# Decode attention with paired key/value heads: fixed on-chip buffers, values one step behind keys, keys turned by column quarters

## The chip, the cores and the metric

The kernel runs on one core of a Trainium2 chip. The metric is the device time of one launch in microseconds (us). Engines of the core that matter here: PE (TensorE, matmuls), DVE (VectorE), ACT (ScalarE), POOL (GpSimd) and SP (SyncE), whose instruction stream issues nearly all the DMAs. Sixteen DMA engines carry the transfers from the chip's memory (HBM) into the on-chip memory (SBUF); matmul results land in PSUM.

## The reference

One decode step. Eight batches, each with one token of width 512, 32 query heads and 8 key/value heads of width 128, a cache of 8192 tokens. All in float32. The sum of three parts is returned:

```python
xn = _layernorm(x)
return x + _A_ref(xn, A_k_cache, A_v_cache, A_wq, A_wo) + _B_ref(xn, B_w1, B_b1, B_w2, B_b2)

# A: grouped-query attention over the cache, four query heads to a key/value head
q = (x @ wq) ...
scores = einsum("bhqd,bhkd->bhqk", q, k) * Dh ** -0.5
o = einsum("bhqk,bhkd->bhqd", softmax(scores), v)
return o ... @ wo

# B: a token-mixing MLP with one token: per batch, 512 channels x 1792 hidden units
u = gelu(einsum("bsd,sf->bdf", layernorm(x), w1) + b1)
return einsum("bdf,fs->bds", u, w2) + b2
```

The two caches are 8 x 8 x 8192 x 128 float32 each, 268 MB for K and as much for V; every byte is read once. The weights wq and wo are 8.4 MB each.

## The kernel before

**Tiles.** The eight key/value heads of each batch are worked on in two ways. Heads 0 to 5 go in pairs: a "duo" is one batch and two neighbouring heads, 24 of them (`N_PR`), and its K and its V are 8.4 MB each, laid out as 128 partitions x 64 KB (64 partitions to a head, each with 128 consecutive tokens). Heads 6 and 7 go one by one: 16 single tiles of 4.2 MB for K and for V each (128 partitions x 32 KB). `slots` (L56) is the buffer for all of them: five slots (`RING`) of 32 KB per partition, so a duo tile takes two slots and a single tile one.

**Slots before.** `slot(n)` (L59) hands the five slots out in a ring, in the order of the loads. A duo tile whose turn comes at the last slot is split: one half in slot 4, one half in slot 0. The weight wq comes first: its main part (`body`) lies in slots 0 and 1, the rest (`extra`) in slot 4.

**Loads.** `load_next` (L184) issues the next load: first the duos (`load_duo`, L166) in the order K0, V0, K1, V1, ..., then the single heads in the order of the list `order`. A duo's load is one DMA with rows of 64 KB or several with shorter rows: K0 comes in four parts of 16 KB rows, the later K duos up to number 7 in two parts of 32 KB rows, from number 8 (`AHEAD`) in one part except every fifth, V duos in one part, and any duo that is split over slots 4 and 0 in two DMAs of 32 KB rows. All are issued by SP, in order, and SP waits before each one until the slot's last reader is done. POOL issues some small parts of wq at the start (`load_side`), and w1, b1, w2 after them.

**A duo step** (`duo_step`, L697) does for one duo i, in the order in which the engines get their instructions:

1. For each half k of the keys (one slot each) and each half of that half: two transposes on DVE in place (`turn_duo`, L570: a chunk of 16 tokens x 128 columns, contiguous, in 32 x 32 blocks), then eight matmuls (`qk_duo`, L576), each over one chunk and one column quarter of 32, which go over two column groups of PE in turn. After the first half `load_next` is called.
2. `softmax_duo` (L588): row maximum on DVE, its transpose over the partitions on PE, the bias on DVE, exp on ACT, two matmuls with `send` and two DVE transposes that bring the weights into `PT`.
3. `pv_duo(i, 0)`: 16 matmuls with the first half of the values, over four column groups; then `load_next`, two pieces of the mixer MLP (`mix`: ACT gelu, POOL multiply and add), and every fourth step the placing of four finished results (`place_duo`); in two steps of eight a projection with wo and its next load.
4. `pv_duo(i, 1)`, the copy of the result out of PSUM on ACT (`take_duo`), two more mixer pieces, and a small exp on ACT that loads its table.

So a step works on K(i) and V(i) together. Each matmul on float32 shows as two instructions in the profile.

**Single heads.** `pair(i)` (L738) turns the keys of head i, and does QK of the one before and PV of the one before that. The last three are written out by hand; the last V comes in five pieces.

**Start.** wq, K0 and the first part of wo are loaded; DVE turns K0; `q_project` (L377) multiplies with wq, main part first and the rest after it, and `q_place_duo` lays the queries into Z. Then the steps begin.

Of the kernel before, what the change touches and what calls it, by code (L numbers as in the profile page):

```python
# [15 lines left out]
REP = HQ // HKV  # L16
# [23 lines left out]
AHEAD = 8  # L40
# [10 lines left out]
def attn_mixer_kernel(ctx: ExitStack, tc: tile.TileContext, x, kc, vc, wq, wo, w1, b1, w2, b2, out):  # L51
# [5 lines left out]
    taken = [0]  # L57

    def slot(n=1):  # L59
        at = taken[0] % RING  # L60
        taken[0] += n
        return slots[:, at:at + n, :]
# [24 lines left out]
    order.sort(key=lambda o: -o[0])  # L87
    at = [o[1:] for o in order].index((kc, KR, N_IT - 1))
    order[at], order[at + 1] = order[at + 1], order[at]
# [6 lines left out]
    body = slot(2).rearrange("p s m -> p (s m)")  # L96
    extra = slots[:, RING - 1, :]
# [66 lines left out]
    duo = [(src, to, i) for i in range(N_PR) for src, to in ((kc, KP), (vc, VP))][::-1]  # L164

    def load_duo():  # L166
        src, to, i = duo.pop()
        g, b = divmod(i, B)
        rows = src[b, 2 * g:2 * g + 2].rearrange("h (p t) d -> (h p) (t d)", p=HP)
        half = NT * DH  # L170
        if taken[0] % RING < RING - 1:
            t = slot(2).rearrange("p s m -> p (s m)")
            n = 1 if to is VP or i >= AHEAD and i % RING else 2 if i else 4
            for a in range(n):
                x = slice(a * 2 * half // n, (a + 1) * 2 * half // n)
                nc.sync.dma_start(t[:, x], rows[:, x])
            parts = [t[:, k * half:(k + 1) * half] for k in range(2)]
        else:
            parts = [slot().rearrange("p s m -> p (s m)") for _ in range(2)]
            for k in (0, 1) if i else (1, 0):  # L180
                nc.sync.dma_start(parts[k], rows[:, k * half:(k + 1) * half])
        to[i] = [t.rearrange("p (t d) -> p t d", d=DH) for t in parts]

    def load_next():  # L184
        if duo:
            load_duo()
        elif order:
            _, src, to, i = order.pop()
            h, b = divmod(i, B)
            t = slot().rearrange("p s (t d) -> p (s t) d", d=DH)  # L190
            rows = src[b, h].rearrange("(p t) d -> p t d", p=P)
            last = not order
            at = 0
            for n in PIECES if last else (NT,):
                nc.sync.dma_start(t[:, at:at + n, :], rows[:, at:at + n, :])
                at += n
            to[i] = t
            if last:
                load_wo(HKV - 1)
# [20 lines left out]
    yrow = const.tile([W, D], F32, name="yrow")  # L220
    load_next()
# [155 lines left out]
    def q_project():  # L377
        part = [[(lw[:, j, :], body[:, j * WB:(j + 1) * WB]) for j in range(a * WJ // 2, (a + 1) * WJ // 2)] for a in range(2)]
        part.append([(lx[:, j, :], extra[:, j * WB:(j + 1) * WB]) for j in range(WE * NB)])
        ms = [misc(), misc()]  # L380
        n = sum(map(len, part))
        at = 0
        for todo in part:
            for a in range(2):
                for j, (l, w) in enumerate(todo, at):
                    g = j % NB
                    nc.tensor.matmul(ms[a][g * W:(g + 1) * W, :], l, w[:, a * REP * DH:(a + 1) * REP * DH],  # L387
                                     start=(j < NB), stop=(j >= n - NB))
# [181 lines left out]
    def turn_duo(i, c):  # L570
        k = KP[i][c // NCH][:, c % NCH * CH_T:(c % NCH + 1) * CH_T, :].rearrange("p t d -> p (t d)")
        nc.vector.transpose(k, k)  # L572
# [3 lines left out]
    def qk_duo(i, k, cs):  # L576
        b = i % B
        if not k and not cs[0]:
            SD[i] = ps_a.tile([P, 512], F32, name="acc")
        t = KP[i][k]  # L580
        for q in range(NB):
            for c in cs:
                nc.tensor.matmul(SD[i][c * W:(c + 1) * W, :].rearrange("p (t j) -> p t j", j=W),  # L583
                                 Z[:, q, b, (1 - k) * REP:(1 - k) * REP + W],
                                 t[:, c * CH_T:(c + 1) * CH_T, q * W:(q + 1) * W],
                                 start=(not k and not q), stop=(k == 1 and q == NB - 1))

    def softmax_duo(i):  # L588
        b = i % B
        s = SD.pop(i)  # L590
        mr = work.tile([P, 1], F32, name="mr")
        nc.vector.tensor_reduce(mr, s, AX.X, ALU.max)  # L592
# [7 lines left out]
        nc.scalar.activation(p, s, AF.Exp, bias=nb, scale=SCALE, accum_out=LD[i // HB][:, b % HB:b % HB + 1])  # L600
# [88 lines left out]
    for c in range(NCH):  # L689
        turn_duo(0, c)  # L690
# [6 lines left out]
    def duo_step(i):  # L697
        g, b = divmod(i, B)
        half = NCH // 2
        for k in range(2):  # L700
            for x in range(2):
                for c in range(half) if i or k else ():
                    turn_duo(i, k * NCH + x * half + c)
                qk_duo(i, k, range(x * half, (x + 1) * half))
            if not k:
                load_next()
                if i == N_PR - 1:
                    load_next()
        if i == N_PR - 1:
            load_next()  # L710
        del KP[i]
        softmax_duo(i)
        pv_duo(i, 0)
        load_next()
        mix(2)
        if b == B - 1 and g < PAIRED // 2 - 1:
            q_place_duo(g + 1)
        if i:
            place_duo(i - 1)
# [5 lines left out]
        if g and b == 2:  # L725
            load_wo(2 * g)
        pv_duo(i, 1)
        if i == N_PR - 1:
            load_next()
        del VP[i]  # L730
        take_duo(i)
        mix(2)
        nc.scalar.activation(small.tile([P, 1], F32, name="warm"), own[:, :1], AF.Exp)  # L733

    for i in range(N_PR):
        duo_step(i)

    def pair(i):  # L738
# [7 lines left out]
        if i == FIRST:  # L746
            place_duo(N_PR - 1)
            fill_softmax(False, big())
            fill_place(False, big())
# [23 lines left out]
        if step[0] <= B * NF:  # L773
            mix(1)
        if h == PAIRED and b == 1:
            o_project(h - 2)
            load_wo(h - 1)
# [70 lines left out]
    assert not order  # L848
# [27 lines left out]
```

## Time and profile before

| | us |
|---|---|
| median of three timed runs | 1292.58 (1291.95 to 1292.74) |
| span of the profiled execution, first to last instruction | 1290.3 |
| PE busy in it | 931.9 (72%) |
| DVE busy | 712.1 (55%) |
| ACT, POOL busy | 236.6, 235.3 (18% each) |
| bytes moved | 554.43 MB, mean 430 GB/s over the span |
| chain that ended last: DMA, PE, DVE | 58%, 20%, 20% |

How to read it. A row such as "PE" under the slices has one digit for each fortieth of the span: the busy share in tenths, 9 being 90% or more. "Idle before" of a group of instructions is how long its engine stood still ahead of them, with what ended the wait. The chain of waits is followed back from the last instruction, at each step to what released it; a piece of it that is a DMA says only that somebody waited from that DMA's issue to its landing. A transfer that is queued behind another is in that time too.

### The profile page before, as it was taken

How to read it: one execution, taken by the hardware profiler on the slowest of the kernel's cores; microseconds unless marked ns; L12 is line 12 of the kernel's file. 1: busy time of each engine (PE TensorE's matmuls, PEld its weight loads, DVE VectorE, ACT ScalarE, POOL GpSimd, SP SyncE). 2: the span in 40 equal slices, each digit the busy share in tenths (PEclk: the TensorE clock that was granted, in tenths of full speed). 3: DMA queues.
4: the chain of work that ended last, by engine and by line, in shares of the span. 5: the costliest groups of instructions: out<-in, count | busy, mean ns of one | idle time of the engine just before them, and what ended most of it. 6: DMA issues, size and time to landing. Idle time of an engine off the chain costs nothing.

```text
span 1290.3 us, 11358 instructions
## 1 busy us (share of the span) xinstructions
PE 931.9 (72%) x4776; PEld 254.5 (20%) x4776; DVE 712.1 (55%) x645; ACT 236.6 (18%) x348; POOL 235.3 (18%) x254
## 2 busy tenths in 40 slices
PE   4677686877786857786848787857687674766778
PEld 1212121212221211121212111212112111111223
DVE  6654446654446634665625665626566645566575
ACT  1022212122111221111221212220223332310000
POOL 3022212122121221112221212220233311100000
PEclk8888898988988979898989898988898887878889
DMA  9999999999999999999999999999999999999998
GB/s 392 434 438 437 429 426 433 434 432 445 422 436 427 432 443 431 428 440 428 429 443 431 426 441 433 425 439 435 425 433 431 433 431 433 431 435 431 431 435 344
DMA packets 17974, 554.43 MB, mean 430 GB/s; under 512 B 2597, under 2 KB 2629, under 8 KB 3409
## 3 DMA queue, kind: packets, MB, share of 16 engines
q1 hardware_dynamic: 17220, 553.08, 99.4%
q8 instruction: 37, 0.61, 0.2%
q0 software_dynamic: 672, 0.61, 0.1%
q14 instruction: 13, 0.11, 0.0%
q10 hardware_dynamic: 32, 0.02, 0.0%
HBM read 553.69 MB, written 0.02 MB: 429 GB/s over the span
## 4 chain that ended last, share of the span: by engine, by line
DMA 58%; PE 20%; DVE 20%; issue 1%; ACT 1%; SPq 0%; POOL 0%; ACTq 0%; DVEq 0%
DMA raw<-in_A_k_cache_dram 39%; DMA raw<-in_A_v_cache_dram 16%; DVE raw L572 14%; PE acc L615 5%; PE acc L583 5%; DVE raw L428 3%; PE acc L506 3%; DMA raw<-in_A_wq_dram 3%; PE misc L603 1%; PE misc L560 1%; PE acc L439 1%; PE misc L632 1%; PE misc L387 0%; ACT t2k L600 0%; DVE s L638 0%
## 5 line engine op out<-in xcount | busy, mean ns | idle before, releaser
L572 DVE STREAM_TRANSPOSE raw<-raw 128x2048 f32<-128x2048 f32 x192 | 425.1, 2275 | 166.3 <-DMA raw<-in_A_k_cache_dram 166.3
L583 PE MATMUL acc<-raw,z 128*32 128x512 f32 x1536 | 396.3, 640 | 165.3 <-DVE raw L572 159.1
L667 POOL TENSOR_SCALAR g<-g,pad 128x512 f32<-128x512 f32 x112 | 77.5, 692 | 720.1 <-ACT g L666 720.1
L615 PE MATMUL acc<-raw,pt 128*32 128x512 f32 x1536 | 189.4, 633 | 14.2 <-DMA raw<-in_A_v_cache_dram 13.3
L583 PEld LDWEIGHTS acc<-raw,z 128*32 128x32 f32 x1536 | 92.4, 115 | 468.3 <-issue 296.7
L428 DVE STREAM_TRANSPOSE raw<-raw 128x2048 f32<-128x2048 f32 x64 | 145.7, 2293 | 65.8 <-DMA raw<-in_A_k_cache_dram 65.8
L668 POOL TENSOR_TENSOR macc<-macc,g 128x512 f32<-128x512 f32 x112 | 142.1, 1269 | 9.3
L666 ACT ACTIVATE g<-hb,pad 128x512 f32<-128x512 f32 x112 | 87.2, 778 | 145.3 <-POOL macc L668 125.3
L600 ACT ACTIVATE t2k<-acc,nb 128x512 f32<-128x512 f32 x24 | 16.5, 687 | 441.7 <-DVE nb L596 441.6
L439 PE MATMUL acc<-raw,z 128*32 128x512 f32 x512 | 82.9, 650 | 10.8 <-DVE raw L428 8.2
L603 PE MATMUL misc<-t2k,send 128*128 128x512 f32 x96 | 62.4, 785 | 33.3 <-ACT t2k L600 33.3
L615 PEld LDWEIGHTS acc<-raw,pt 128*32 128x32 f32 x1536 | 51.9, 115 | 149.8 <-issue 121.7
L506 PE MATMUL acc<-raw,pt 128*32 128x512 f32 x480 | 75.9, 772 | 0.0
L604 DVE STREAM_TRANSPOSE pt<-misc 128x512 f32<-128x512 f32 x48 | 34.4, 717 | 69.3 <-PE misc L603 67.6
L592 DVE TENSOR_REDUCE mr<-acc 128x1 f32<-128x512 f32 x24 | 16.6, 692 | 89.1 <-PE acc L583 89.1
L456 PE MATMUL misc<-ident,mr 128*128 128x128 f32 x16 | 6.4, 398 | 76.3 <-DVE mr L451 76.3
L666 ACT ACT_TABLE_LOAD x32 | 41.1, 1283 | 29.0 <-PE hb L658 28.5
L623 ACT COPY ob<-acc 128x512 f32<-128x512 f32 x24 | 14.0, 584 | 150.5 <-PE acc L615 150.5
L473 ACT ACTIVATE t2k<-acc,nb 128x512 f32<-128x512 f32 x16 | 11.0, 687 | 134.7 <-DVE nb L462 134.6
L439 PEld LDWEIGHTS acc<-raw,z 128*32 128x32 f32 x512 | 19.5, 117 | 64.0 <-issue 44.8
L733 ACT ACT_TABLE_LOAD x24 | 30.8, 1283 | 0.4
L603 PEld LDWEIGHTS misc<-t2k,send 128*128 128x128 f32 x96 | 19.6, 226 | 52.8 <-ACT t2k L600 37.8
(136 smaller groups left out, 375.8 us busy)
## 6 DMA issues: line engine op xcount, KB each, us to landing
raw<-in_A_k_cache_dram SPq DMA_DIRECT2D x44, 4096.0 KB, 32.8
raw<-in_A_v_cache_dram SPq DMA_DIRECT2D x25, 4096.0 KB
raw<-in_A_k_cache_dram SPq DMA_DIRECT2D x4, 2048.0 KB, 17.4
raw<-in_A_wq_dram SPq DMA_DIRECT2D x2, 3584.0 KB, 13.3
wo<-in_A_wo_dram SPq DMA_DIRECT2D x7, 1024.0 KB
raw<-in_A_v_cache_dram SPq DMA_DIRECT2D x3, 1024.0 KB
raw<-in_A_v_cache_dram SPq DMA_DIRECT2D x2, 512.0 KB, 25.5
wo<-in_A_wo_dram SPq DMA_DIRECT2D x4, 256.0 KB
```

The source lines that it names most:

```text
L428: nc.vector.transpose(k, k)
L439: nc.tensor.matmul(S[i][c * W:(c + 1) * W, :].rearrange("p (t j) -> p t j", j=W), Z[:, q, b, REP:], k[:, c * CH_T:(c + 1) * CH_T, q * W:(q ...
L506: nc.tensor.matmul(O[i][j * W:(j + 1) * W, :].rearrange("p (c d) -> p c d", c=NCH), pt[:, t * W:(t + 1) * W], v[:, t], start=(t < NB), sto ...
L572: nc.vector.transpose(k, k)
L583: nc.tensor.matmul(SD[i][c * W:(c + 1) * W, :].rearrange("p (t j) -> p t j", j=W), Z[:, q, b, (1 - k) * REP:(1 - k) * REP + W], t[:, c * C ...
L603: nc.tensor.matmul(m, send[:, k, :], p, start=True, stop=True)
L604: nc.vector.transpose(PT[k][:, :CH_T * W], m)
L615: nc.tensor.matmul(OD[i][j * W:(j + 1) * W, :].rearrange("p (c d) -> p c d", c=NCH), PT[k][:, t * W:(t + 1) * W], v[:, t], start=(not k an ...
L666: nc.scalar.activation(g, hb, AF.Gelu_apprx_tanh, bias=b1t[:, j:j + 1], scale=w1t[:, j:j + 1])
L667: nc.gpsimd.tensor_scalar(g, g, w2t[:, j:j + 1], 1.0, op0=ALU.mult, op1=ALU.mult)
L668: nc.gpsimd.tensor_add(acc, acc, g)
L733: nc.scalar.activation(small.tile([P, 1], F32, name="warm"), own[:, :1], AF.Exp)
```

## The change

The five slots are no longer a ring while duos are worked on. Keys have slots 0 to 2: duo i lies in slots 0 and 1 or in slots 1 and 2, in turn, so that two neighbouring duos share slot 1 (`home`; K1 alone lies in 2 and 3). Values have slots 3 and 4 (V0 in 4 and 0). At the start wq lies in slots 2, 3 and 4, so K0 gets slots 0 and 1. A list, `plan`, gives the order of the loads: K0 in two DMAs, K1, V0 in two DMAs, then K2, V1, K3, V2, ..., K23, V22, the first single K, V23, and the other single heads. Every duo from K1 and V1 on is one DMA of 8.4 MB with rows of 64 KB. The half of the keys that lies in slot 1 is worked on first, and K(i+1) is asked for right after it. The single heads then use the slots in the fixed round 2, 1, 0, 3, 4.

The values are worked on a step later: step i does QK of duo i, and PV, `take_duo` and the asking for the next V for duo i-1; `place_duo` is for duo i-2. PV's first half stands between the row maximum and its transpose over the partitions, the second half between exp and the matmuls with `send`. The four mixer pieces come together at the end of the step. V23 is worked on in the first `pair`.

The keys are turned by column quarters: one transpose takes 32 of the 128 columns over all 64 tokens of a partition in one half (64 runs of 32 elements), and is followed by the four matmuls of that quarter, one for each column group. The number of transposes and of matmuls is the same.

```diff
-    duo = [(src, to, i) for i in range(N_PR) for src, to in ((kc, KP), (vc, VP))][::-1]
...
+    def home(i):
+        return 2 if i == 1 else 1 - i % 2 if i else 0
+
+    plan = [(kc, KP, 0, (0,), (0,)), (kc, KP, 0, (1,), (1,)), (kc, KP, 1, (2, 3), (0, 1)),
+            (vc, VP, 0, (4,), (0,)), (vc, VP, 0, (0,), (1,))]
+    for i in range(1, N_PR - 1):
+        a = home(i + 1)
+        plan.append((kc, KP, i + 1, (a, a + 1), (0, 1)))
+        plan.append((vc, VP, i, (3, 4), (0, 1)))
+    plan.append(order[0])
+    plan.append((vc, VP, N_PR - 1, (3, 4), (0, 1)))
+    plan += order[1:]
+    plan.reverse()
...
+            t = slot(at[0], len(at)).rearrange("p s m -> p (s m)")
+            nc.sync.dma_start(t, rows[:, part[0] * half:(part[-1] + 1) * half])
...
-    def turn_duo(i, c):
-        k = KP[i][c // NCH][:, c % NCH * CH_T:(c % NCH + 1) * CH_T, :].rearrange("p t d -> p (t d)")
-        nc.vector.transpose(k, k)
+    def turn_duo(i, k, q):
+        t = KP[i][k][:, :, q * W:(q + 1) * W]
+        nc.vector.transpose(t, t)
...
+    def qk_duo(i, k, q, first):
...
+        for c in range(NCH):
+            nc.tensor.matmul(SD[i][c * W:(c + 1) * W, :].rearrange("p (t j) -> p t j", j=W),
+                             Z[:, q, b, (1 - k) * REP:(1 - k) * REP + W],
+                             t[:, c * CH_T:(c + 1) * CH_T, q * W:(q + 1) * W],
+                             start=(first and not q), stop=(not first and q == NB - 1))
...
+    def values_duo(i, k):
+        pv_duo(i, k)
+        if k:
+            del VP[i]
             load_next()
...
+    def duo_step(i):
+        g, b = divmod(i, B)
+        for k in (1, 0) if i > 1 and i % 2 else (0, 1):
+            first = k == (i > 1 and i % 2)
+            for q in range(NB):
+                if i or k:
+                    turn_duo(i, k, q)
+                qk_duo(i, k, q, first)
+            if first:
+                load_next()
+        del KP[i]
+        mr = top_duo(i)
+        if i:
+            values_duo(i - 1, 0)
+        p = exp_duo(i, mr)
+        if i:
+            values_duo(i - 1, 1)
+        send_duo(p)
+        if b == B - 1 and g < PAIRED // 2 - 1:
+            q_place_duo(g + 1)
+        if i > 1:
+            place_duo(i - 2)
+        project_duo(g, b)
+        if i:
+            take_duo(i - 1)
+        mix(4)
         nc.scalar.activation(small.tile([P, 1], F32, name="warm"), own[:, :1], AF.Exp)
...
+        if i == FIRST:
+            pv_duo(N_PR - 1, 0)
+            load_next()
+            values_duo(N_PR - 1, 1)
+            take_duo(N_PR - 1)
+            place_duo(N_PR - 1)
+            fill_place(False, big())
```

More of the change, by code (lines that the diff above doesn't have):

```diff
@@ L163, in attn_mixer_kernel @@
     HP = P // 2
-    duo = [(src, to, i) for i in range(N_PR) for src, to in ((kc, KP), (vc, VP))][::-1]
[L166 to L182, printed above, removed]
@@ new lines, in attn_mixer_kernel @@
+    plan = [(kc, KP, 0, (0,), (0,)), (kc, KP, 0, (1,), (1,)), (kc, KP, 1, (2, 3), (0, 1)),
[8 more added lines that the diff above has]
+    plan.reverse()
+    def load_next():
+        if not plan:
+            return
+        src, to, i, at = plan[-1][:4]
+        if to is KP or to is VP:
+            part = plan.pop()[4]
+            g, b = divmod(i, B)
+            half = NT * DH
+            rows = src[b, 2 * g:2 * g + 2].rearrange("h (p t) d -> (h p) (t d)", p=HP)
+            t = slot(at[0], len(at)).rearrange("p s m -> p (s m)")
+            nc.sync.dma_start(t, rows[:, part[0] * half:(part[-1] + 1) * half])
+            for n, k in enumerate(part):
+                to.setdefault(i, {})[k] = t[:, n * half:(n + 1) * half].rearrange("p (t d) -> p t d", d=DH)
+            return
+        plan.pop()
+        h, b = divmod(i, B)
+        t = slot(at).rearrange("p s (t d) -> p (s t) d", d=DH)
+        rows = src[b, h].rearrange("(p t) d -> p t d", p=P)
+        last = not plan
+        at = 0
+        for n in PIECES if last else (NT,):
+            nc.sync.dma_start(t[:, at:at + n, :], rows[:, at:at + n, :])
+            at += n
+        to[i] = t
+        if last:
+            load_wo(HKV - 1)
@@ L687, in mix @@
                 mx_step(b, j)
-    for c in range(NCH):
-        turn_duo(0, c)
+    for q in range(NB):
+        turn_duo(0, 0, q)
     q_project()
@@ L695, in attn_mixer_kernel, with project_duo @@
     nc.vector.tensor_copy(yrow, m[:W, :])
[L697 to L709, printed above, removed]
-            load_next()
[L711 to L719, printed above, removed]
+    def values_duo(i, k):
+        pv_duo(i, k)
+        if k:
+            del VP[i]
+            load_next()
+    def project_duo(g, b):
         if g and b == 1:
```

70 lines of the change are left out of this document (23 added, 47 removed).

## The prediction

> **What bounds the kernel now.** I read the page's slices first, then its queues.
>
> ```profile
> PE   4677686877786857786848787857687674766778
> DVE  6654446654446634665625665626566645566575
> DMA  9999999999999999999999999999999999999998
> GB/s 392 434 438 437 429 426 433 434 432 445 422 436 427 432 443 431 428 440 428 429 443 431 426 441 433 425 439 435 425 433 431 433 431 433 431 435 431 431 435 344
> DMA packets 17974, 554.43 MB, mean 430 GB/s; under 512 B 2597, under 2 KB 2629, under 8 KB 3409
> q1 hardware_dynamic: 17220, 553.08, 99.4%
> ```
>
> The DMA engines are busy in every slice, PE and DVE are not; SP's queue (q1) alone fills 99.4% of the sixteen engines' span. So no wait of PE or DVE sets the end, although the chain of waits is full of them. The end is: bytes over rate, plus a head before the first packet, a tail after the last, and every moment in which an engine's queue is empty. The tail is the chain's last part:
>
> ```profile
> 1258.43 25.54 DMA raw<-in_A_v_cache_dram
> ...
> 1284.01 0.69 PE acc L516 x16
> ```
>
> After the last piece of V lands at 1284.0 the span runs 6.3 us more, to 1290.3; the timed runs (median 1292.58) carry 2.3 us more than the profiled span. Bytes, head and tail are not touched by the change (the list of single heads keeps its order, only its slots are named otherwise). What can move is the rate and the empty moments. The rate by stage, in the windows (us, then busy times, granted clock, DMA share, GB/s):
>
> ```profile
> 0.00:47.00 47.00, 20.57 (x111) 6.90 (x111) 28.09 (x115) 6.65 (x7) 11.60 (x22) 0.85 0.98 404
> 107.00:361.00 254.00, 194.58 (x927) 52.34 (x928) 135.74 (x90) 48.27 (x70) 54.11 (x57) 0.89 1.01 434
> 438.00:940.00 502.00, 371.08 (x1767) 95.63 (x1766) 266.44 (x189) 91.90 (x131) 101.27 (x106) 0.89 1.00 433
> 990.00:1230.00 240.00, 155.51 (x872) 42.59 (x870) 143.46 (x125) 45.98 (x69) 29.59 (x31) 0.82 1.00 433
> ```
>
> From 107 us on it is full: 434 with most key pairs in two halves, 433 with mostly whole pairs, 433 with single heads. A pair tile (8.39 MB) takes 8.39/0.433 = 19.4 us, a step (K and V) 38.8, a single head 9.7.
>
> **The change, part by part.**
>
> *Rows of 64 KB.* Before, of 24 K pairs 9 come whole, 14 in halves, one in quarters; of 24 V pairs 19 whole, 5 in halves:
>
> ```profile
> raw<-in_A_k_cache_dram SPq DMA_DIRECT2D x44, 4096.0 KB, 32.8
> raw<-in_A_v_cache_dram SPq DMA_DIRECT2D x25, 4096.0 KB
> raw<-in_A_k_cache_dram SPq DMA_DIRECT2D x4, 2048.0 KB, 17.4
> raw<-in_A_v_cache_dram SPq DMA_DIRECT2D x19, 28.6
> raw<-in_A_k_cache_dram SPq DMA_DIRECT2D x9, 35.6
> ```
>
> (Of the first row's 44, 16 are single heads; of the second's 25, 15.) After, all but K0 and V0 come whole: 18 tiles go from 32 KB rows to 64 KB rows, K0 from 16 KB to 32 KB, and 20 DMAs fall away. The trace's packet records, counted by size:
>
> ```
> size      count  us each
> 65536 B    3584  2.418
> 32768 B    8843  1.213
> 16384 B     583  0.611
> 8192 B     1299  0.309
> 4 B        2444  0.009
> first packet of the run at 1.78 us (its DMA issued at 0.74)
> the first wo load's 128 packets of 8 KB start between 39.54 and 48.49 us
> ```
>
> Two packets of 32 KB cost 2 x 1.213 - 2.418 = 0.008 us more than one of 64 KB. 18 x 128 x 0.008 / 16 engines = 1.15 us; K0 gives 256 x 0.009 / 16 = 0.15; 20 completion writes less per engine, 20 x 0.009 = 0.2. Sum **-1.5 us**. The windows bound it by rounding: two stages that differ by at most 2 GB/s in 433 over 18 x 19.4 = 349 us allow 1.6 us, and nothing at the other end.
>
> In the Trainium skill, "SBUF — State Buffer", section "The DMA setup-cost knee", every transfer pays about 2 us whatever its size. By it 20 DMAs less would be an estimated 40 us, a time near 1253. The rows above speak against it: loads of 4 MB and of 8 MB move at one rate. I keep it as a rival below.
>
> *Quarters by column.* 192 transposes before and after, 2048 elements each; the matmuls stay 1536 but go over four column groups in turn, not two:
>
> ```profile
> L572 DVE STREAM_TRANSPOSE raw<-raw 128x2048 f32<-128x2048 f32 x192 | 425.1, 2275 | 166.3 <-DMA raw<-in_A_k_cache_dram 166.3
> L583 PE MATMUL acc<-raw,z 128*32 128x512 f32 x1536 | 396.3, 640 | 165.3 <-DVE raw L572 159.1
> L615 PE MATMUL acc<-raw,pt 128*32 128x512 f32 x1536 | 189.4, 633 | 14.2 <-DMA raw<-in_A_v_cache_dram 13.3
> ...
> 518.26 17.68 DVE raw L572 x8
> 535.98 3.63 PE acc L583 x14
> 539.64 0.70 DVE mr L592
> ...
> 545.72 3.57 PE acc L615 x32
> ```
>
> L615 already goes over four groups: 32 in 3.57 us, where two groups of L583 take 3.63 for 16. So QK's busy time should fall from 396 towards L615's 189 us, and what is left after the last transpose from 3.63 to 8/32 x 3.57 = 0.9. Worth nothing to the end: PE waits for DVE and DVE for DMA. No row shows a transpose over 64 runs of 32 elements; the nearest bounds are the contiguous 2275 ns and, for a strided operand, L638's reduce beside L592's over as many elements:
>
> ```profile
> L592 DVE TENSOR_REDUCE mr<-acc 128x1 f32<-128x512 f32 x24 | 16.6, 692 | 89.1 <-PE acc L583 89.1
> L638 DVE TENSOR_REDUCE s<-t2k 128x32 f32<-128x512 f32 x6 | 6.6, 1102 | 0.2
> ```
>
> a factor of 1.59. I take 2275: the runs stay 32 long, which is what one turned block reads, while L638 steps at every element.
>
> *Fixed buffers, values a step behind.* This is what could empty the queue. Let S be the time at which a step's keys are through the DMA engines; V(i-1), 19.4 us, is behind them. DVE starts at S+0.4, four turns take 8.9 and the last quarter 0.9, so **K(i+1) is issued at S+10.2, needed at S+19.4**. QK ends at 0.4 + 17.7 + 0.9 = S+19.0; V(i-1) is there at S+19.8; two halves of PV follow, with the row-max transpose (0.4) between them. One half took 3.6 to 5.4 us in the chain, on average 189.4/48 = 3.95. **V(i) is issued at S+28.2 (27.4 to 31.1), needed at S+38.8.** Behind the V wait on SP stand only the next K (due 20 us later) and in two steps of eight a wo load. On PE the row-max transpose and the sends now queue behind PV's wait for V(i-1), and exp and the PT transposes wait for those; they are done by about S+32, before the next keys at S+38.8. ACT and POOL run four mixer pieces in a row, off the path. With margins of 9 to 11 us the cost is 0; without them each us late would be a us of time.
>
> *Last pair step.* K48 is half as long, so V23 is due at S+19.4+9.7 = S+29.1; issued at S+28.2 plus 1.04 from issue to first packet, it is **0.2 us late** (0 to 3.0). Afterwards K49 and V48 stand in the queue, 19.4 us, while V23 is used.
>
> *Start.* From the timeline and the chain: SP's issues, the projection's main part, POOL's last piece of wq from its issue at 26.54, the projection's rest and the first QK:
>
> ```profile
> 14.01 1.77 SPq L176 DMA_DIRECT2D raw<-in_A_k_cache_dram  x4
> ...
> 30.84 14.69 SPq L181 DMA_DIRECT2D raw<-in_A_v_cache_dram  x2
> 45.58 9.48 SPq L176 DMA_DIRECT2D raw<-in_A_k_cache_dram  x2
> ...
> 26.12 5.55 PE L387 MATMUL misc<-raw,ob 128*32 128x512 f32 x28 [5.57 <-DMA raw<-in_A_wq_dram]
> 26.54 12.77 DMA raw<-in_A_wq_dram
> ...
> 39.40 5.79 PE misc L387 x32
> ...
> 49.31 8.62 PE L583 MATMUL acc<-raw,z 128*32 128x512 f32 x50 [0.18 <-ACT z L406]
> ```
>
> K1 now goes where the main part of wq lay; that is read by 26.12 + 5.55 = 31.7, so K1 is issued near 32, and V0's first half where the rest of wq lay, after the projection. But POOL's pieces of wq share the engines with K0, and in the records packets of the two queues alternate one for one. K0's packets now last 1.21 us, not 0.61. Counting turns on the engine that ended last (22 of POOL's items behind 16 of K0's packets, then wo's short ones) the rest of wq lands 8 us later and the projection resumes at E = 47.4, not 39.4 (39.4 to 52.1, the latter if all of the 12.77 us doubles). QK follows at E+9.9; On DVE K0's other half starts at E+10.4; its turns (8.9), the rest of its QK and the softmax up to the PT transposes (0.9 + 6.5; the chain has 6.1 from 539.64 to 545.72), K1's first half (8.9) and its QK (1.1) put K2's issue at E+36.7 = 84.1, first packet 85.1. The queue then holds K1 and V0: 17.85 MB until 44.4 (by the first window), 16.78 MB more, so 83 to 84 for the mean engine. The engines don't run in step: wo's eight packets each, 2.2 us in step, start over 8.95, so the slowest engine is some 2.6 us behind the mean and has work until about 86.5. The slowest sets the end; cost **0** (0 to 3.3).
>
> Sum: 1292.58 - 1.5 + 0.2 = **1291.3 us**.
>
> **The rivals.** *Late start (slower).* If E passes 48.7, the slowest engine too runs dry before K2, and every us of E is a us of time. For it: DVE is serial from the projection to K2, nothing can overtake. Against: E moves only if POOL's items are queued all along. At E = 52 and the mean engine's bound, 3 to 6 us; taken at 4.5: 1295.8. In the Trainium skill, "DMA: Bandwidth & Descriptors", section "Queues, rings and completion order", an engine takes turns between queues at packet granularity, a packet being many descriptors; by whole bundles POOL's items would wait longer and the sum would be this rival's 1295.8; the records here alternate row by row.
>
> *Dearer turns (slower).* At 1.59 x 2275 ns eight turns take 28.9 us, 11.2 more. V(i)'s first packet then comes at S+40.4, 1.7 us after its queue is empty; a late V delays the next K by as much, so this is paid in every second step: 20 us, with some 11 at the last pair step and 9 at the start about 1331. It decides from (38.8 - 29.2)/8 = 1.2 us more per turn on. Against it: the 32-long runs.
>
> *Paid setup (faster).* If every load paid a start of its own in series, fewer loads would pay fewer. By the rows this is small: the 25 loads of 4 MB in the window from 990 to 1230 us cost at most 2 GB/s of 433, 1.1 us, so 0.045 us each; 20 of them 0.9 us, 1290.4. The Trainium skill's 2 us (page and section above) would give 1253, less than the 1277 us that 554.43 MB need at 434 GB/s alone.
>
> *Nothing moves.* The rows' 1.5 us is lost to the late start: 1292.6, inside the forecast's class.
>
> **How the numbers follow.** 0.2% (2.6 us) is about what a measurement of this kernel can tell from no change. Forecast with "nothing moves" 0.73 (its own range 1289.9 to 1294.5); late start 0.15; dearer turns 0.05; faster 0.07, of which paid setup 0.01 and the rest an end at which the slowest engine is nearer to the mean (they lie some 3 us apart). Below 1290.0 counts as faster, above 1295.2 as slower. The range 1289.8 to 1296.5 takes in the gain's bound and most of the late start, and leaves the dearer turns and the far end out.
>
> **What would show it.** Right: DMA at 9 in every slice but the last, q1 near 15,000 packets, L583's successor near 190 us, transposes at 2.28 us, K issued 9 us before its queue ends. Late start: the projection's last part after 48.7, a slice below 430 GB/s near 85 us. Dearer turns: the transposes' mean, and dips in each step. The forecast is wrong if the DMA row has a slice under 9 between 100 and 1280 us, or if the head or tail moved.

## The result, and the profile after

The changed kernel takes 1300.61 us (median, 1299.85 to 1301.28), the kernel before 1292.33 beside it: a ratio of 1.0064, interval 1.0053 to 1.0075, so 8.3 us slower. The forecast was 1291.3 in a range that ended at 1296.5. The profiled execution has a span of 1298.8 us.

The slices and the main queue of the changed kernel's page:

```profile
DMA  9989999999999999999999999999999999999997
GB/s 391 435 360 430 429 442 425 441 432 434 428 436 430 432 439 430 439 428 428 441 426 445 424 441 424 439 428 441 430 403 426 430 435 433 433 427 431 435 435 336
DMA packets 15093, 554.42 MB, mean 427 GB/s; under 512 B 2277, under 2 KB 2309, under 8 KB 3089
q1 hardware_dynamic: 14340, 553.08, 98.7%
```

Two slices stand out, the third (360 GB/s, where there was 438) and the thirtieth (403, where there was 433). The queue has fewer packets for the same bytes and fills a smaller share of a longer span. The windows of the changed kernel (us, busy times of PE, PEld, DVE, ACT, POOL, granted clock, DMA share, GB/s) show where it is empty:

```profile
47.00:107.00 60.00, 47.46 (x270) 12.48 (x270) 31.91 (x24) 12.64 (x20) 8.40 (x9) 0.77 0.91 390
60.00:100.00 40.00, 28.64 (x159) 5.78 (x155) 29.61 (x19) 7.94 (x10) 7.91 (x9) 0.78 0.88 376
80.00:90.00 10.00, 6.30 (x40) 0.83 (x40) 10.00 (x6) 3.82 (x5) 6.93 (x8) 0.83 0.60 231
107.00:940.00 833.00, 487.09 (x2940) 106.12 (x2939) 443.99 (x312) 158.92 (x225) 175.70 (x182) 0.82 1.00 433
940.00:990.00 50.00, 25.51 (x164) 6.55 (x165) 25.61 (x19) 12.03 (x21) 11.76 (x12) 0.72 0.96 411
955.00:970.00 15.00, 10.20 (x81) 3.91 (x77) 6.50 (x10) 4.20 (x6) 3.60 (x4) 0.94 0.93 390
```

and the same of the kernel before:

```profile
47.00:107.00 60.00, 44.20 (x223) 12.19 (x222) 32.48 (x24) 12.28 (x19) 10.21 (x11) 0.94 1.01 434
107.00:940.00 833.00, 623.54 (x2959) 163.34 (x2963) 441.48 (x309) 153.10 (x219) 169.12 (x177) 0.89 1.00 433
```

Between 107 and 940 us, the pair steps, both move 433 GB/s: as far as the rounding tells, the change costs and brings nothing there. Against 433 the first row of the changed kernel lacks (433 - 390)/433 x 60 = 6.0 us, the last 1.5. The start and the last pair step so hold 7.5 of the 8.3 us. The chain of waits of the changed kernel at the start (start, us, what):

```profile
28.07 19.80 DMA raw<-in_A_wq_dram
...
47.96 6.39 PE misc L391 x32
...
60.16 8.81 DVE raw L577 x4
...
78.22 8.86 DVE raw L577 x4
...
87.12 1.11 PE acc L587 x8
...
88.25 21.73 DMA raw<-in_A_k_cache_dram
```

The last piece of wq takes 19.80 us from issue to landing, where it took 12.77. The projection's rest begins at 47.96, K0's second half is turned from 60.16, K1's first half from 78.22, and only then, at 88.25, is K2 asked for. The trace's packet records tell how many rows the sixteen DMA engines have under way at a time: sixteen until 80.5, nine at 82, eight at 84.5, four at 86, none after 88.1. K2's first packet starts at 89.2. Averaged over the engines, 5.6 us are empty. The chain at the last pair step:

```profile
935.67 17.67 DVE raw L577 x8
...
958.91 3.62 PE acc L624 x32
...
962.54 22.64 DMA raw<-in_A_v_cache_dram
```

V23 is asked for at 962.54, when both halves of PV of pair 22 are done, and the queue has run low by then: in the packet records the first engines run dry at 960, eight still work when V23's first packet starts at 963.5, and the last has rows of its own until 965.4. Averaged over the engines, 1.8 us are empty.

### The profile page after: what moved, and what is told of

Same layout as the page of the kernel before. It is cut to its first block, busy times and chain, and to the rows that moved or that the text cites. A ratio compares the mean times of both kernels' runs of the same rounds, so it can differ in the third digit from the quotient of the medians.

```text
span 1298.8 us, 11285 instructions
## 1 busy us (share of the span) xinstructions
PE 782.8 (60%) x4776; PEld 191.4 (15%) x4776; DVE 710.9 (55%) x645; ACT 238.8 (18%) x348; POOL 235.5 (18%) x254
## 4 chain that ended last, share of the span: by engine, by line
DMA 65%; DVE 17%; PE 15%; issue 1%; ACT 1%; POOL 0%; SPq 0%; ACTq 0%; DVEq 0%
DMA raw<-in_A_k_cache_dram 41%; DMA raw<-in_A_v_cache_dram 21%; DVE raw L577 13%; PE acc L624 6%; DMA raw<-in_A_wq_dram 3%; PE acc L511 3%; DVE raw L433 3%; PE acc L587 2%; PE acc L444 1%; PE misc L641 1%; PE misc L391 0%; PE misc L612 0%; DVE mr L456 0%; PE misc L565 0%; PE misc L681 0%
## 5 line engine op out<-in xcount | busy, mean ns | idle before, releaser
L577 DVE STREAM_TRANSPOSE raw<-raw 128x2048 f32<-128x2048 f32 x192 | 423.9, 2274 | 160.6 <-DMA raw<-in_A_k_cache_dram 160.6
L587 PE MATMUL acc<-raw,z 128*32 128x512 f32 x1536 | 272.6, 794 | 332.5 <-DVE raw L577 331.4
L624 PE MATMUL acc<-raw,pt 128*32 128x512 f32 x1536 | 177.9, 604 | 31.0 <-DMA raw<-in_A_v_cache_dram 31.0
L587 PEld LDWEIGHTS acc<-raw,z 128*32 128x32 f32 x1536 | 35.0, 122 | 564.8 <-DVE raw L577 362.9
L444 PE MATMUL acc<-raw,z 128*32 128x512 f32 x512 | 74.7, 619 | 5.9 <-DVE raw L433 5.9
L511 PE MATMUL acc<-raw,pt 128*32 128x512 f32 x480 | 75.7, 769 | 0.0
L602 DVE CUSTOM_DVE_ANT_0 t2k<-misc,hmask 128x128 f32<-128x128 f32 x24 | 7.0, 292 | 87.7 <-PE misc L600 87.7
L612 PE MATMUL misc<-t2k,send 128*128 128x512 f32 x96 | 49.3, 637 | 2.7 <-ACT t2k L606 2.7
L391 PE MATMUL misc<-raw,ob 128*32 128x512 f32 x88 | 17.7, 924 | 25.0 <-DMA raw<-in_A_wq_dram 25.0
```

Source lines behind the costliest of these rows:

```text
L444: nc.tensor.matmul(S[i][c * W:(c + 1) * W, :].rearrange("p (t j) -> p t j", j=W), Z[:, q, b, REP:], k[:, c * CH_T:(c + 1) * CH_T, q * W:(q ...
L511: nc.tensor.matmul(O[i][j * W:(j + 1) * W, :].rearrange("p (c d) -> p c d", c=NCH), pt[:, t * W:(t + 1) * W], v[:, t], start=(t < NB), sto ...
L577: nc.vector.transpose(t, t)
L612: nc.tensor.matmul(m, send[:, k, :], p, start=True, stop=True)
L624: nc.tensor.matmul(OD[i][j * W:(j + 1) * W, :].rearrange("p (c d) -> p c d", c=NCH), PT[k][:, t * W:(t + 1) * W], v[:, t], start=(not k an ...
```

## The experiments

The theory: the time goes at those two places, because a load is asked for too late. Its first form (theory A) names the length of K0's rows, behind which POOL's small pieces of wq wait. The rivals: the time goes with the rows themselves, the turns or the later values. Each ratio is against the kernel before, run on the same chip beside it.

**K0 in shorter rows, and in longer ones.** Two edits of the changed kernel, each alone: K0 in four DMAs of 16 KB rows, and K0 in one DMA of 64 KB rows.

```diff
+            n = 2 if to is KP and not i else 1
+            for a in range(n):
+                o, e = a * half // n, (a + 1) * half // n
+                if n > 1:
+                    nc.sync.dma_start(t[:, o:e], rows[:, part[0] * half + o:part[0] * half + e])
...
```

```diff
-    plan = [(kc, KP, 0, (0,), (0,)), (kc, KP, 0, (1,), (1,)), (kc, KP, 1, (2, 3), (0, 1)),
+    plan = [(kc, KP, 0, (0, 1), (0, 1)), (kc, KP, 1, (2, 3), (0, 1)),
...
-    load_next()
     load_next()
     load_wo(0)
```

> The changed kernel with K0 loaded in four DMAs of 16 KB rows, as the kernel before had it; all else as changed. Theory A (late start: POOL's last part of wq waits behind K0's 32 KB packets, so the projection and with it K2's load come too late): the projection's last part starts near 40 us instead of 47.96, K2 is issued near 80 instead of 88.25, the window from 80 to 90 us rises from 231 GB/s to about 430, and the time falls by the 5.6 us of that window to some 1295 us. Theory B (the loss is in the pair steps or at V23): 1300.6 us, within 1 us. Theory C (DVE's serial work up to K2 sets the hole and wq does not): the projection comes earlier but K2 is still issued near 88, 1300.6 us.

> The changed kernel with K0 in one DMA of 64 KB rows. Theory A: the packets of K0 last 2.42 us instead of 1.21, the 22 turns of POOL's last items end later; 8 turns behind K0, 8 behind wo, some 6 behind K1's packets, so the projection resumes near 60 us instead of 48 and the hole before K2 grows by as much: some 1312 us (1308 to 1316). Theory C: no change of K2's issue, 1300.6 us. Theory B: 1300.6 us.

16 KB: 1294.48, ratio 1.0017 (1.0008 to 1.0026). 64 KB: 1310.70, 1.0141 (1.0127 to 1.0155), inside the expected range. The chain with 64 KB rows:

```profile
30.35 28.37 DMA raw<-in_A_wq_dram
58.81 5.71 PE misc L390 x32
...
98.35 21.76 DMA raw<-in_A_k_cache_dram
```

The chain with 16 KB rows, and its window from 60 to 100 us:

```profile
31.13 37.60 DMA raw<-in_A_k_cache_dram
68.82 8.90 DVE raw L583 x4
77.76 1.11 PE acc L593 x8
78.89 28.46 DMA raw<-in_A_k_cache_dram
```

```profile
60.00:100.00 40.00, 26.39 (x140) 5.82 (x140) 21.84 (x18) 11.60 (x16) 9.82 (x10) 0.83 1.00 431
```

The same piece of wq takes 12.77 us with 16 KB rows (in the kernel before), 19.80 with 32 KB and 28.37 with 64 KB, and K2 is asked for at 78.89, 88.25 and 98.35. Here and below, E is the time at which the projection's rest begins (47.96 in the changed kernel). In the 16 KB chain wq's last piece is gone: K1's landing at 68.7 starts the turn. So with an early E it is the queue itself that sets K2's issue, and the stretch from 60 to 100 us moves 431 GB/s where the changed kernel has 376.

**K0 in rows of 8 KB** (with V23 in two DMAs, below; `n = 4` in the line above), to see whether earlier still is better:

> The kernel with V23 in two DMAs and K0 in rows of 8 KB instead of 16 KB: POOL's small items wait 0.31 us a turn instead of 0.61, E falls from 40 to about 36 and K2 is issued near 75 instead of 79. If the start costs time only as far as K2 comes after the queue is empty (a threshold that 16 KB rows already keep): no gain, 1292.8 within 0.7. If every us by which the start comes earlier is a us of time: 1289.

1293.63, ratio 1.0008 (0.9999 to 1.0017), against 1292.81 with 16 KB: no gain. The timeline of PE has E at 33.56, that of SP has K2 no earlier than before:

```profile
33.56 3.64 PE L398 MATMUL misc<-raw,ob 128*32 128x512 f32 x32 [1.00 <-issue]
```

```profile
79.66 0.33 SPq L194 DMA_DIRECT2D raw<-in_A_k_cache_dram  x1
```

The expected 75 was wrong for the reason just seen, K1's landing. An earlier E alone brings nothing; whether an earlier K2 would is not tested by this run, since K2 came no earlier.

**The kernel before with K0 in rows of 32 KB:**

```diff
-            n = 1 if to is VP or i >= AHEAD and i % RING else 2 if i else 4
+            n = 1 if to is VP or i >= AHEAD and i % RING else 2
```

> The kernel before with K0 in two DMAs of 32 KB rows instead of four of 16 KB; all else as before. Theory A: the projection's last part moves from 39.4 to some 48 us here too, since the same packets stand ahead of POOL's. If the ring of the kernel before has slack (its half tiles are asked for one by one, its first half of V0 at 30.8), the time stays at 1292.5 us within 1; if the long packets alone make the loss, whatever the buffers, it goes to some 1298 us.

1296.94, ratio 1.0032 (1.0019 to 1.0045): 4.6 us for this alone, between the two times that were expected. The chain has the same piece of wq, and two windows are thin:

```profile
27.88 19.89 DMA raw<-in_A_wq_dram
```

```profile
48.00:56.00 8.00, 8.00 (x49) 3.30 (x46) 0.38 (x1) 1.17 (x2) 0.00 (x0) 0.67 0.85 351
47.00:107.00 60.00, 51.96 (x270) 15.35 (x270) 32.02 (x24) 13.45 (x21) 9.28 (x11) 0.84 0.98 413
```

Against the 434 of the kernel before, the second lacks 2.9 us, of which the first has 1.5; where the rest of the 4.6 us goes is not shown. There the late loads are others: V0's second half, which waits for the slot in which wq's rest lies, and K1 behind it on SP. A late E goes with a longer time in both kernels, by whichever load waits for it.

**wq's rest ahead of K0, on SP's queue.** The changed kernel with K0's 32 KB rows, V23 in two DMAs, and the small pieces issued by SP instead of POOL:

```diff
-        nc.gpsimd.dma_start(pad[:n, at:at + 3:2].unsqueeze(2), wq[:n, 0:3:2].unsqueeze(2))
+        nc.sync.dma_start(pad[:n, at:at + 3:2].unsqueeze(2), wq[:n, 0:3:2].unsqueeze(2))
...
+    load_side()
...
     make_identity(nc, ident)
-    load_side()
...
```

> The changed kernel with K0 in rows of 32 KB as it is and V23 in two DMAs, but the twelve small loads of wq's rest issued by SP ahead of K0 instead of by POOL beside it, so that they share no engine with K0's packets. If the late start is the wait of POOL's small items behind K0's long packets: the rest is there before the projection's main part ends, E is near 32 instead of 48, K2 is issued near 72, the slice from 60 to 100 us has 430 GB/s, and the time is that of the kernel with 16 KB rows for K0, 1292.8 (up to 1294 if the twelve items lie unevenly on the engines). If long rows of K0 cost something by themselves (the rival): 1292.58 + 4.6 or more as in the kernel before with 32 KB rows, 1297 to 1299.

1307.19, ratio 1.0115 (1.0101 to 1.0128). It does not settle the question. The first window shows why:

```profile
0.00:47.00 47.00, 20.41 (x110) 7.63 (x110) 18.70 (x110) 6.65 (x7) 4.62 (x10) 0.82 0.68 272
```

SP stood still between the last of the small pieces (issued at 16.8, 24.8, 29.6 and 34.5 us) and issued K0 only at 35.2, not at 14; the queue was empty for much of that time. At 272 GB/s, where the kernel before has 404, some 14 us are lost there. K2 is asked for at 91.93, 3.7 us later than in the changed kernel, and from 47 to 107 us nothing is empty (435 GB/s): the whole queue lies later, so K2 is no longer late against it.

**K2 in two DMAs, K0's rows left at 32 KB.** What remained open is whether K0's rows are the cause or K2's being one DMA, which waits for both of its slots. In the kernel before, K2 was in two halves.

```diff
+            full = len(at) * half
+            n = 2 if to is KP and i == 2 else 1
+            for a in range(n):
+                o, e = a * full // n, (a + 1) * full // n
+                nc.sync.dma_start(t[:, o:e], rows[:, part[0] * half + o:part[0] * half + e])
```

> The changed kernel with K2 alone in two DMAs of 32 KB rows; K0 keeps its 32 KB rows. If the hole is there because one DMA waits for both of K2's slots: the first half waits for the keys of duo 0 in slot 1 only, is issued near 70 (the last QK of duo 0 in the changed kernel's chain ends at 70.1), brings 9.7 us of work before the queue is empty near 84, the second half follows near 88 in time, the stretch from 60 to 100 us has 430 GB/s, E is still near 48, and the time is that of the kernel with 16 KB rows for K0, 1294.5. If K0's long rows or the late E cost the time whatever K2 does: 1300.6.

1295.24, ratio 1.0020 (1.0011 to 1.0029): 5.4 us of the 8.3 are gone. E, in PE's timeline, and the two halves of K2, in SP's (a group's time reaches from the start of the first issue to the end of the last, and one issue takes 0.33 us):

```profile
47.86 6.35 PE L395 MATMUL misc<-raw,ob 128*32 128x512 f32 x32 [16.26 <-DMA raw<-in_A_wq_dram]
```

```profile
70.03 18.45 SPq L191 DMA_DIRECT2D raw<-in_A_k_cache_dram  x2
```

```profile
60.00:100.00 40.00, 26.95 (x167) 5.76 (x159) 29.51 (x19) 7.94 (x10) 7.88 (x8) 0.87 0.99 426
```

E is as late as in the changed kernel, 47.86, and yet the stretch is nearly full, 426 GB/s for 376: the first half goes out at 70.03, when duo 0 is done with slot 1, and its 9.7 us of work cover the wait for the second, issued near 88.15. So two things together make the hole, and either one removed closes it (by the packet records, 0.3 us of empty engines stay with K2 in two, none with 16 KB rows): a late E, and one DMA that waits for two slots.

**V23.** Four runs bear on the second hole. First, K49 asked for ahead of V23, alone (s2) and with K0 in 16 KB rows (s3):

```diff
-    plan.append(order[0])
+    plan += order[:2]
     plan.append((vc, VP, N_PR - 1, (3, 4), (0, 1)))
-    plan += order[1:]
+    plan += order[2:]
...
             if first:
                 load_next()
+                if i == N_PR - 1:
+                    load_next()
...
     for i in range(N_PR):
         duo_step(i)
-    load_next()
     load_next()
```

> The changed kernel with K49 asked for ahead of V23 (its slot is free by then), so that 9.7 us more stand in the queue when V23 is issued. Theory B (the empty queue before V23 costs what the windows lack there): the window from 955 to 970 us rises from 390 to about 430 GB/s and the time falls by 1.7 us to 1298.9. Theory A with the slowest engine never empty there: the window fills but the time stays at 1300.6 us, within 0.5.

> Both edits: K0 in 16 KB rows and K49 ahead of V23. If the two holes are all that was lost, what is left is the longer rows' gain of 1.5 us less 0.15 for K0: 1291.0 us, below the kernel before (1292.3). If more was lost elsewhere in the steps, 1293 us or above.

Both missed: 1302.92 (1.0078, 1.0065 to 1.0092) and 1296.13 (1.0024, 1.0015 to 1.0033), each some 2 us worse than without the edit. The windows of s2, and its chain:

```profile
955.00:970.00 15.00, 10.17 (x81) 3.88 (x77) 6.62 (x10) 4.21 (x6) 3.64 (x4) 0.95 1.02 440
990.00:1040.00 50.00, 34.57 (x178) 9.72 (x182) 22.66 (x26) 6.43 (x9) 6.41 (x7) 0.77 0.95 392
```

```profile
962.50 32.22 DMA raw<-in_A_v_cache_dram
994.86 9.24 PE acc L624 x64
```

The hole at 955 is filled, but V23 now lands 32.22 us after its issue instead of 22.64, its PV ends 10 us later, and the loads that wait for its slots leave a larger hole at 990. Then V23 in two DMAs, with K0 in 16 KB rows, the first asked for after PV's first half (s8):

```diff
-    plan.append((vc, VP, N_PR - 1, (3, 4), (0, 1)))
+    plan.append((vc, VP, N_PR - 1, (3,), (0,)))
+    plan.append((vc, VP, N_PR - 1, (4,), (1,)))
...
         if k:
             del VP[i]
+        if k or i == N_PR - 2:
             load_next()
```

> The changed kernel with K0 in 16 KB rows, and V23 in two DMAs of 4 MB, the first asked for after PV's first half, some 4 us earlier than V23 was; nothing else stands ahead of it. Theory B (V23's late issue costs about a us): the dip at 955 to 970 us goes and nothing comes in its place later, unlike with K49 ahead; 1294.5 less 0.5 to 1.7: 1293 to 1294. If the slowest engine was never empty there: 1294.5.

1292.81, ratio 1.0004 (0.9995 to 1.0013): level with the kernel before, 1.7 us under the same kernel with V23 whole (1294.48). Last, the two splits alone, K2 and V23, with K0's 32 KB rows and every request where the change has it (`or to is VP and i == N_PR - 1` added to the line `n = 2 if ...` of the run with K2 in two, s14):

> The same with V23 in two DMAs of 32 KB rows as well, both still asked for at the same place in the code. If V23's hole too is a wait for two slots at once: the first half is issued some 4 us earlier, when PV's first half is done, 940 to 990 us has 430 GB/s, and the time is 1292.8, level with the kernel before. If the place in the code matters: 1294.5, as the run above.

1293.62, ratio 1.0009 (1.0000 to 1.0019). SP's timeline and the window:

```profile
952.25 4.16 SPq L191 DMA_DIRECT2D raw<-in_A_v_cache_dram  x2
```

```profile
940.00:990.00 50.00, 32.76 (x215) 9.81 (x215) 23.05 (x26) 12.60 (x22) 11.75 (x12) 0.86 0.99 429
```

The first half is issued some 3.8 us before the second (4.16 less the 0.33 of one issue), without any move in the code: SP waits for one slot's reader instead of two. From 940 to 990 us there are 429 GB/s, where the changed kernel has 411. The time lies between the two that were expected, and 1.6 us under s14, which is what s8 gained by the moved request; so the place in the code did not matter, as far as these times tell (s8 has K0 in shorter rows too).

**The turns, by contiguous chunks again** (the changed kernel with the transposes and QK loops of the kernel before):

```diff
-    def turn_duo(i, k, q):
-        t = KP[i][k][:, :, q * W:(q + 1) * W]
+    def turn_duo(i, k, c):
+        t = KP[i][k][:, c * CH_T:(c + 1) * CH_T, :].rearrange("p t d -> p (t d)")
...
```

> The changed kernel with the keys turned by chunks of 16 tokens again, two column groups at a time in QK; buffers, order of loads and the values' step as changed. Theory A: what is left of QK after the last turn of a half grows from 1.1 to some 3.7 us; twice on the way to K2, once on the way to V23: K2 5 us later, V23 2.6 us later, 1305 to 1308 us. A theory in which the turns by column cost time: 1299 us or less.

1306.01, ratio 1.0104 (1.0090 to 1.0118): the column quarters are worth 5.4 us in the changed kernel. Its group of QK, beside the changed kernel's three groups (busy, mean ns):

```profile
L588 PE MATMUL acc<-raw,z 128*32 128x512 f32 x1536 | 405.5, 656 | 221.3 <-DVE raw L577 213.6 <-issue 7.1 <-ACT z L411 0.2
```

```profile
L577 DVE STREAM_TRANSPOSE raw<-raw 128x2048 f32<-128x2048 f32 x192 | 423.9, 2274 | 160.6 <-DMA raw<-in_A_k_cache_dram 160.6
L587 PE MATMUL acc<-raw,z 128*32 128x512 f32 x1536 | 272.6, 794 | 332.5 <-DVE raw L577 331.4
L624 PE MATMUL acc<-raw,pt 128*32 128x512 f32 x1536 | 177.9, 604 | 31.0 <-DMA raw<-in_A_v_cache_dram 31.0
```

The turn costs the same (2274 ns, 2275 before); what is shorter is QK after the last turn (1.11 us for 3.63 in the chains), which lies on the way to K2 and to V23. That is not the whole account of the 5.4 us, although the time came out as expected. K2 is asked for at 90.06, only 1.8 us later than in the changed kernel, where 5 were expected, because the rest of the chain ran faster there (the four matmuls with `send` take 2.00 us for 3.68). Against the changed kernel the windows lack 1.1 us from 47 to 107 (382 GB/s), 1.3 from 940 to 990 (400), and some 2 in the pair steps between (432 for 433, which rounding leaves uncertain by as much). Why the steps lose is not shown.

**The rows.** Every pair tile in two DMAs of 32 KB rows, with K0 in 16 KB rows (s9); the same with V23 asked for as in s8 (s10); and with 16 KB rows (s11, four for each whole pair and two for a half):

```diff
+            n = 2 if len(at) == 2 else 2 if to is KP and not i else 1
+            full = len(at) * half
+            for a in range(n):
+                o, e = a * full // n, (a + 1) * full // n
+                nc.sync.dma_start(t[:, o:e], rows[:, part[0] * half + o:part[0] * half + e])
```

> The changed kernel with K0 in 16 KB rows and every later pair tile in two DMAs of 32 KB rows, issued one behind the other. Rows of 64 KB are worth 0.008 us per 64 KB on each engine: 44 tiles x 128 rows x 0.008 / 16 = 2.8 us by the packets' durations, so 1294.5 + 2.8 = 1297.3 us. If the long rows give nothing in sum (other packets get longer as these get shorter): 1294.5 us. If long rows cost: below 1294.

> The kernel with K0 in rows of 16 KB and V23 in two DMAs (1292.81 us, no engine dry between 60 and 1250 us in its trace), with every pair tile from K1 and V1 on in two DMAs of 32 KB rows. Neither kernel has an empty moment, so this is the price of the rows alone. If two 32 KB packets cost 0.008 us more than one of 64 KB on the path that sets the end (the prediction's term): 45 tiles x 128 x 0.008 / 16 = 2.9 us and some 44 completion writes of 0.009 = 0.4, 1296.1. If rows are worth nothing because the time a shorter packet costs is taken from waits inside the others: 1292.8, within 0.7.

> The same with every pair tile in rows of 16 KB, a larger dose. If the packets' own durations add up: 45 x 128 x (4 x 0.611 - 2.418 = 0.026) / 16 = 9.4 us and 3 x 44 x 0.009 = 1.2, so 1303.4. If rows are worth nothing: 1292.8, within 0.7.

1293.88 (1.0011, 1.0002 to 1.0020), 1293.81 (1.0011, 1.0002 to 1.0020) and 1298.00 (1.0043, 1.0029 to 1.0057). s9 is no clean pair with the kernel with K0 in 16 KB rows (s1, 1294.48): it also splits V23, which its expectation left out and which gains about what the rows cost. The clean pairs are s10 and s11 against s8 (1292.81): +1.0 us for 32 KB rows where 2.9 to 3.3 were computed from the packets, +5.2 for 16 KB where 10.6 were. The sums of the packets' durations did rise as computed, but the span did not follow:

```
kernel   packets' durations / 16   span      span less sum
s8       1285.97                   1290.3     4.3
s10      1289.00                   1291.7     2.7
s11      1296.57                   1296.0    -0.6
```

With 16 KB rows the durations add to more than the span, although its head and tail move nothing: packets of one engine overlap. A third (s10) to a half (s11) of the packets' extra duration reaches the end. The windows of s10 and s11:

```profile
107.00:940.00 833.00, 512.38 (x2935) 108.16 (x2931) 439.36 (x309) 154.46 (x220) 168.88 (x175) 0.79 1.00 433
```

```profile
107.00:940.00 833.00, 501.28 (x2923) 109.49 (x2923) 435.18 (x308) 155.29 (x220) 169.25 (x176) 0.80 1.01 431
```

The 45 more DMAs of s10 (45 more completion writes on each engine) cost 1.0 us in all, 0.02 each. In the Trainium skill, "SBUF — State Buffer", section "The DMA setup-cost knee", each transfer pays about 2 us, most of it completion latency. In the span of these runs it does not show, as long as the queue holds further loads.

## Why the prediction was wrong, step by step

The account by parts: changed kernel 1300.6; K2 split 5.4 us; V23 split 1.6; what is left, 1293.6, is 1.1 us above the kernel beside it (0.0 to 2.5 by the interval), and that rest has no cause shown.

**The start, put at 0 (0 to 3.3): the step that failed, by 5.4 to 6.1 us.** Three of its parts:

- E was right: 47.4 forecast, 47.96 in the trace, from the packets that alternate.
- The chain from E to K2 was mis-sized: E+36.7 forecast, 88.25 - 47.96 = 40.3 measured. K0's second half is turned from E+12.2, not E+10.4, and from the end of that turn (68.97) to the next turn (78.22) it takes 9.25 us, not 7.4. The durations came from the kernel before, where PE's granted clock was 0.94 from 47 to 107 us; here it is 0.77. By the timelines the extra time is PE's: the projection's rest takes 6.39 us for 5.75, the two matmuls of L703 1.91 for 1.04, the four with `send` 3.67 for 1.98.
- The slack was not there. The mean engine's queue was forecast to end at 83 to 84, which the 231 GB/s between 80 and 90 us bear out; the forecast then allowed the slowest engine to work until 86.5 and let it alone set the end. With K2's first packet 1.04 us after its issue, at 89.3, that reading gives 2.8 us and the mean engine's 5.3 to 6.3. In the packet records the slowest engine even works until 88.1, some 4.3 us behind the mean, so that it stands empty for 1.1 us only, while the mean is 5.6. Measured were 5.4 (K2 split) and 6.1 (16 KB rows). So the mean engine's gap was paid, and the slowest engine's work was no slack. With 64 KB rows the same reckoning, 98.35 + 1.04 less 84, gives 15.4 us; against 16 KB rows 16.2 were measured.

Behind it stands a thing not seen at all: K2 was taken as a single event, although the two slots it needs come free 18 us apart (70.03 and 88.15 with K2 in two) and the kernel before asked for its halves one by one. The step on rows counted what fewer DMAs save and not that a merged one waits for the later of two readers.

**The late start, given 0.15, was the right rival**, with the right mechanism and sign. Of its two signs one came, a slice below 430 GB/s near 85 us, and one did not: E > 48.7 was named as the point of decision, and E was 47.96. In the trace K1's turn begins at E+30.3 (78.22), K2's issue is 10.0 later and its first packet 1.0 after that: E+41.3. With the queue's end near 84, E costs time, by this estimate, from 84 - 41.3 = 42.7 on; below about 38.4, K1's landing at 68.7 sets K2 and E no longer matters. Its price of 4.5 us was near the measured 5.4 to 6.1; the 1295.8 also held a gain of 1.5 that did not come and only 0.2 for V23.

**V23, put at 0.2 (0 to 3.0):** 1.6 to 1.7 us measured, by two pairs of runs. The bound held, the central value did not. The request was not late by its own clock: the first turn (S+0.4) starts at 935.67, so 962.54 is S+27.3, where S+28.2 was forecast. What was wrong is the time at which it is due, S+29.1. S is the landing that DVE sees, that of the slowest engine; the mean engine is ahead of it and runs dry sooner. With the first packet at S+28.3 and 1.7 us lost it is dry at S+26.6, some 2.5 us ahead, about the 2.6 that the prediction had worked out for this lag at the start. The packet records bear it out: when V23's first packet starts, half of the engines are still at work, the slowest never runs dry, and the mean over the engines is 1.8 us empty.

**The rows, put at -1.5 us:** the sign may be right, the size is about half at most. By s10 a third of the computed price showed, by s11 a half: -0.5 to -0.7 for the 18 tiles, which no run here can tell from nothing. The sum took a packet's duration for its price, and packets overlap.

**Fixed buffers and values a step behind, put at 0:** right. 433 GB/s from 107 to 940 us in both kernels. **Column quarters, put at 0 in steady steps:** right for the turn, 2274 ns, so the dearer turns did not come. QK was forecast near 190 us and is 272.6, with 794 ns a matmul where PV has 604. In PE's timeline the eight instructions behind one turn take 1.06 us or up to 1.93 (around 510 us); why was not tried. In the pair steps no cost of it shows. What was not said is that the quarters shorten the way to K2 and V23: without them the changed kernel is 5.4 us slower (s6), of which the windows place 1.1 us at K2 and 1.3 at V23.

**Paid setup** did not come either (0.02 us for each added load, by s10).

## What to carry to other kernels

When loads are merged, write down for each which reader it now waits for: a single DMA into two buffers starts when the later one comes free, which was harmless in the steady steps, with some 9 us of margin, and cost 5.4 and 1.6 us at their two ends. Take durations for a stage from a place with the same granted clock, and don't let an engine that happens to lag stand in for slack. Here a small load on one queue came later the longer the rows of the other queue were; keep rows short beside a small load that something waits for.

## What the runs showed of the hardware that was not expected

- The latency of POOL's last small piece of wq went from 12.77 to 19.80 to 28.37 us as the rows of K0 on SP's queue went from 16 to 32 to 64 KB (packets of 0.611, 1.213 and 2.418 us). In the Trainium skill, "DMA: Bandwidth & Descriptors", section "Queues, rings and completion order", an engine alternates between queues by packets, typically of many descriptors. The trace agrees that it alternates; the grain here is one row, as E, worked out that way, came within 0.6 us.
- PE's granted clock was lower in the changed kernel, where PE had less to do: 0.82 against 0.89 between 107 and 940 us, where PE is busy 487 us against 624. The runs show no cause.
- Durations of packets on one engine can add to more than the time that passes (1296.57 on average over the engines against a span of 1296.0 us with 16 KB rows).
- The sixteen DMA engines of one queue run far out of step: in the changed kernel the first is through with V0 near 81 us, the last at 88.1.
